# The scale of w_in from sums of squares on TensorE instead of maxima on VectorE, in a fused attention and feed-forward kernel

## The chip, the cores and the metric

The kernel runs on one core of one Trainium2 chip. The metric is device time in microseconds (us) of one execution; three executions of the kernel before are given. A core has five engines that run side by side, each through its own list of instructions in a fixed order: TensorE (PE in the profile, with its weight loads as PEld), VectorE (DVE), ScalarE (ACT), GpSimd (POOL) and SyncE (SP, which here only issues DMAs).

## The reference

Attention with a multiplicative forget gate, then a feed-forward layer, 8 batches, 8 heads, 576 positions, head width 64:

```python
scores = q @ k.T / sqrt(64)
cum = cumsum(log(clip(f, 1e-4, 1)))
attn = softmax(where(causal, -1e9, scores + cum[i] - cum[j]))
x = (attn @ v), heads side by side      # 4608 tokens x 512
h = x @ w_in                            # 512 x 1024
s = h * softmax(h)
ln = (s - mean(s)) / sqrt(var(s) + 1e-6) * g_ln
out = ln @ w_out                        # 1024 x 512
```

`w_in` and `w_out` come in 64-bit floats, everything else in 32-bit ones. So a weight is read as two 32-bit words that have to be joined into one 32-bit float.

## The kernel before, in words

**Work.** Attention is done by pairs of heads: 4 pairs per batch, 32 pairs. A pair has five tiles of query rows (i = 0 to 4, the later the longer). Per tile: score products on TensorE (`score_products`, L873, with the decay added by L869 or L871), the row maximum on VectorE (L894), the exponential with its row sum on ScalarE (L899), the reciprocal (L905, L906), the scaled probabilities (L910 or L919, recorded at the helper's line L555 for VectorE and GpSimd and L553 for ScalarE), their transposition (TensorE, L946, for the first batch, by DMA later), and the product with the values (L968 or L973), whose result goes to `x16`. After it, 36 layers of 128 tokens: product with `w_in` into `hps` (L1013), softmax and normalisation (L1022 to L1054), transposition, product with `w_out` (L1079), output. From the second batch on, and in the layers throughout, a 32-bit number is carried as two 16-bit floats, high part and rest, so a product is three passes. In the first batch the attention's products are made in 32 bits.

**The scale.** So that the 16-bit parts don't lose range, each operand is multiplied by a power of two. `scale_w_in` (L673 to L680) finds that of `w_in`: for each of the four chunks (128 x 1024 weights, 1 MB) VectorE takes the largest absolute value of the raw high words as soon as the chunk has landed (L677), then the maximum of the four (L688); TensorE turns that column into a row (L693), VectorE makes the power of two out of it (L699 to L709), TensorE spreads it to all partitions (L718), VectorE finishes it (L723, L724).

**The joining.** `weights` (L620 to L655) joins the words of chunk c: ScalarE moves the high word into place (L634), then, for chunks 0 and 1, ScalarE writes the top bits of the low word into a PSUM buffer (L648) and VectorE joins them in two halves (L654); for chunks 2 and 3 GpSimd makes the top bits (L637) and VectorE joins in one piece (L639). The joined chunk lies in a buffer of the layers (`ets`, `zts`) until it is split into `wi_h` (L665, one of three engines) and `wi_l` (L670, VectorE), which need the scale.

**The order.** Nothing is ordered on the chip. The program lists 3766 operations with their dependencies (`plan.op`); ORDER, written out by hand as numbers, says in which order each engine gets them, and ON says which of the operations that could run on several engines goes to which. An engine never passes a waiting instruction. `Plan.schedule` follows ORDER with a table of costs only to choose PSUM buffers and to find where TensorE would idle in the first 60 us: there L1204 issues products of the identity matrix that nobody reads (fillers below). TensorE uses its array either as a whole, or split by rows (scores) or columns (values, and nearly all layer products).

The operations of the start on TensorE, in order: fillers; scores of pair 0, tiles 0 to 2; fillers; the scale's transposition (L693); scores of pair 1, tiles 0 and 1; transposes of pair 0; L718; scores of pair 1, tile 2 (its products are the 64x320 ones at L873); values of pair 0; and so on to the first layer product (L1013).

The lines that matter:

```python
sw = scales["wi"][:, 1, 0:1]
copied(WI_H[c], {ACT: 1050, DVE: 690, POOL: 1130}, due, wi_h[:, c, :], w, [wk, ("scale", "wi", 0)], [("wi", c)], scale=sw)
```

Of the kernel before, what the change touches and what calls it, by code (L numbers as in the profile page):

```python
# [8 lines left out]
F32 = mybir.dt.float32  # L9
F32R = mybir.dt.float32r  # L10
I32 = mybir.dt.int32
# [4 lines left out]
ALU = mybir.AluOpType  # L16
# [68 lines left out]
class Plan:  # L85
# [140 lines left out]
    def spare(self, a, e):  # L226
# [40 lines left out]
    },  # L267
    DVE: {
# [6 lines left out]
    },  # L275
    POOL: {
        26, 67, 276, 280, 284, 613, 614, 698, 1506, 1524, 1648, 1995, 2190, 2483, 2785, 2882, 2883, 2971, 3043, 3096, 3113, 3114, 3252, 3317, 3400,
        3541, 3621, 3650, 3651, 3690,
# [156 lines left out]
def tile_kernel(ctx: ExitStack, tc: tile.TileContext, qk, v, f, w_in, w_out, g_ln, out):  # L435
# [701 lines left out]

    for p in range(NPAIR):
        load(p, -97.0 + p)
    scale_w_in(WI_SCALE)  # L1140
    load_v(0, HALF[0][0] + VDUE[0])
    for n in range(2):
        squares(0, n, 0, HALF[0][0] + VDUE[1])
# [105 lines left out]
```

## Time and profile before

| | us |
|---|---|
| median of three runs | 632.39 (631.79 to 634.35) |
| the profiled execution's own time | 630.9 |
| its span, first to last instruction | 629.1 |
| TensorE busy | 611.7 (97%) |
| VectorE busy | 570.8 (91%) |
| ScalarE busy | 516.9 (82%) |
| GpSimd busy | 347.7 (55%) |

All times in the rows are us from the start of the span unless marked ns. What lies between the span and the execution's time is 1.8 us. A matmul's record covers its whole way through the array, so records of one engine overlap: a run of equal matmuls takes the distance of their starts, not the sum of their durations. A 32-bit product shows as two records, each with a weight load of its own on PEld.

### The profile page before, as it was taken

To read this page: it belongs to the slowest core of one execution; us is meant where nothing else is said; L and a number is where in the kernel's file an instruction comes from. 1 tells how busy PE (TensorE), PEld (TensorE's weight loads), DVE (VectorE), ACT (ScalarE), POOL (GpSimd) and SP (SyncE) were. 2 spreads that over 40 slices of the span, in tenths; PEclk is the share of its full clock that TensorE was granted. 3 is DMA by queue.
4 is the path that set the end of the run, shared out by engine and by line. 5 is a ranking of instruction groups with operands and counts; after the bars stand their busy time and mean duration, and the time that the engine had idled before them with its cause. 6 is when DMAs were issued, how large, how long until landed. Compare 5 with 4: busy or idle time off the path is not lost.

```text
span 629.1 us, 20473 instructions
## 1 busy us (share of the span) xinstructions
PE 611.7 (97%) x7843; PEld 361.9 (58%) x7843; DVE 570.8 (91%) x1776; ACT 516.9 (82%) x1282; POOL 347.7 (55%) x547
## 2 busy tenths in 40 slices
PE   5899999999999999999999999999999999999997
PEld 4556665565555556555556555556655655655555
DVE  6999999999999999999999999999999999897442
ACT  6999999989989999899988889898898786764122
POOL 5565751585768646666566745664455644444230
PEclk9999999999999999999999999999999999999999
DMA  8767128979989999999999999999978687787541
GB/s 331 271 219 270 39 95 243 155 152 213 210 162 207 188 206 163 214 149 244 187 201 173 254 165 241 200 157 202 170 134 162 124 138 138 120 143 134 112 118 51
DMA packets 262722, 110.99 MB, mean 176 GB/s; under 512 B 248288, under 2 KB 248736, under 8 KB 261600
## 3 DMA queue, kind: packets, MB, share of 16 engines
q1 hardware_dynamic: 262624, 109.69, 83.9%
q8 instruction: 61, 1.00, 0.6%
q14 instruction: 37, 0.30, 0.2%
HBM read 38.27 MB, written 9.66 MB: 76 GB/s over the span
## 4 chain that ended last, share of the span: by engine, by line
PE 58%; DVE 0%; ACT 0%; issue 0%
PE ps L1079 21%; PE hps L1013 20%; PE ps L973 7%; PE ps L873 6%; PE ps L871 2%; PE ps L1093 0%; PE ps L1096 0%; PE ps L1094 0%; PE ps L693 0%; PE ps L1065 0%; PE ps L718 0%; DVE wo_p L927 0%; ACT y L1104 0%; DVE p L894 0%; DVE nm L894 0%
## 5 line engine op out<-in xcount | busy, mean ns | idle before, releaser
L1079 PE MATMUL ps<-wo_f,zz 128*64 128x512 f16 (+1 forms) x1617 | 194.0, 380 | 0.0
L899 ACT ACTIVATE p<-p,nm 128x448 f32<-128x448 f32 (+4 forms) x208 | 133.2, 642 | 15.7 <-DVE nm L894 13.4
L1079 PEld LDWEIGHTS <-zz 128*64 128x64 f16 (+1 forms) x1617 | 91.1, 109 | 84.0 <-issue 6.5
L1013 PE MATMUL hps<-wi_h,x_h 128*64 128x512 f16 (+1 forms) x562 | 111.5, 383 | 1.0 <-DVE e L1028 1.0
L1013 PE MATMUL hps<-wi_l,x_h 128*64 128x512 f16 (+1 forms) x562 | 110.3, 379 | 0.0
L1013 PE MATMUL hps<-wi_h,x_l 128*64 128x512 f16 (+1 forms) x562 | 110.3, 379 | 0.0
L873 PE MATMUL ps<-qk 64*128 64x288 f16 (+9 forms) x1056 | 101.4, 303 | 2.8 <-DMA qk<-in_qk_dram 1.8
L894 DVE CUSTOM_DVE_ANT_0 p<-ps,mask 128x320 f32<-128x320 f32 (+4 forms) x208 | 99.9, 497 | 3.6 <-PE ps L871 1.1
L1013 PEld LDWEIGHTS <-x_h 128*64 128x64 f16 (+1 forms) x1124 | 60.0, 109 | 58.1 <-issue 14.7
L1049 POOL TENSOR_TENSOR z<-e,z 128x512 f16<-128x512 f32 x55 | 66.7, 1222 | 34.2 <-ACT z L553 33.4
L927 DVE SCALAR_TENSOR_TENSOR wo_p<-p,ri,wo_p 128x448 f16<-128x448 f32 (+1 forms) x112 | 84.6, 773 | 0.7 <-ACT wo_p L553 0.3
L973 PEld LDWEIGHTS <-v 128*64 128x64 f16 x2520 | 73.1, 110 | 10.5 <-issue 2.8
L973 PE MATMUL ps<-t_p,v 128*64 128x128 f16 (+1 forms) x2520 | 76.5, 218 | 0.0
L905 POOL TENSOR_SCALAR sm<-sm 128x2 f32<-128x2 f32 (+1 forms) x93 | 29.2, 314 | 80.6 <-ACT p L899 54.9
L1024 ACT ACTIVATE e<-hps,st,unscale 128x1024 f32<-128x1024 f32 x32 | 38.5, 1203 | 27.6 <-DVE st L1023 27.4
L555 POOL TENSOR_SCALAR wo_p<-p,ri 128x576 f16<-128x576 f32 (+1 forms) x43 | 37.4, 871 | 30.4 <-DVE ri L906 21.9
L1022 DVE TENSOR_REDUCE st<-hps 128x1 f32<-128x1024 f32 x36 | 43.8, 1218 | 8.8 <-PE hps L1013 8.2
L871 PE MATMUL ps<-crow,pick 64*128 64x448 bf16 (+1 forms) x360 | 51.4, 276 | 0.0
L873 PEld LDWEIGHTS <-qk 64*128 64x128 f16 x864 | 32.4, 94 | 31.9 <-issue 20.4
L1013 PEld LDWEIGHTS <-x_l 128*64 128x64 f16 (+1 forms) x562 | 32.7, 110 | 29.5
L1036 ACT ACTIVATE junk<-e,st 128x1024 bf16<-128x1024 f32 x36 | 41.3, 1146 | 9.7 <-DVE e L1028 9.5
L1028 DVE SCALAR_TENSOR_TENSOR e<-hps,e 128x1024 f32<-128x1024 f32 x36 | 43.6, 1212 | 4.1 <-ACT e L1024 4.0
(213 smaller groups left out, 1184.5 us busy)
## 6 DMA issues: line engine op xcount, KB each, us to landing
raws<-in_qk_dram SPq DMA_DIRECT2D x24, 576.0 KB, 5.6
vraw<-in_v_dram SPq DMA_DIRECT2D x8, 1280.0 KB, 7.2
out_dram<-y SPq DMA_DIRECT2D x35, 256.0 KB, 3.1
qk<-in_qk_dram SPq DMA_DIRECT2D x8, 576.0 KB, 6.5
wo_raw<-in_w_in_dram SPq DMA_DIRECT2D x4, 1024.0 KB, 8.6
vraw<-in_w_out_dram SPq DMA_DIRECT2D x2, 1024.0 KB, 5.8
t_raw<-in_w_out_dram SPq DMA_DIRECT2D x2, 1024.0 KB, 5.5
t_p<-p16s SPq DMA_TRANSPOSE x84, 3.6
```

What stands on the lines that cost most here:

```text
L871: nc.tensor.matmul(dst, pick[row(h), a2, a1:a1 + 1].broadcast_to([D, P]), crow[row(h), a2, cols], start=False, stop=True)
L873: nc.tensor.matmul(dst, x[row(h), 0, q0:q0 + P], y[row(h), 1, cols], start=(n == 0), stop=False)
L894: op(DVE, R_NS[i] if n == 0 else 442, at[i][h] + STEPS[0], lambda i=i, h=h, n=n, a=a, e=e, x=x, m0=m0: nc.vector.tensor_tensor_reduce(home ...
L899: op(ACT, E_NS[i] + (0 if banked(p, i) or i == 4 else 28), at[i][h] + STEPS[1], lambda i=i, h=h, x=x: nc.scalar.activation(home(i, h), hom ...
L927: op(DVE, L_NS[j], at[j][g] + STEPS[4], lambda j=j, g=g, nq=nq, h16=h16, l16=l16, r1=r1: nc.vector.scalar_tensor_tensor(l16(), home(j, g, ...
L973: nc.tensor.matmul(o[row(h), a:a + n], v16[m][:, x, 2 * j + h], t[:, y, i + j if h else i - j], start=(j == 0 and c == 0), stop=(j == i an ...
L1013: nc.tensor.matmul(hps[k, sl], x[:, k], w[:, c, sl], start=start, stop=stop)
L1022: op(DVE, 1215, at, lambda: nc.vector.tensor_reduce(s[:, 0:1], hps, axis=AX.X, op=ALU.max, negate=True), [("h",)], [("st", n % 2)])
L1028: nc.vector.scalar_tensor_tensor(et, hps, 1.0 / DFF, et, ALU.mult, ALU.mult, accum_out=s[:, 3:4])
L1036: op(ACT, 1140, at, lambda: nc.scalar.activation(junk[:, :DFF], et, AF.Square, bias=s[:, 3:4], scale=-float(DFF), accum_out=s[:, 5:6]), [e ...
L1049: op(POOL, 1085, at, lambda e, a=a: engine(e).tensor_tensor(z16[:, a, 1], e2[:, a], z16[:, a, 0], ALU.subtract), [ek, zk_], [(*zk_, "l", a ...
L1079: nc.tensor.matmul(y[t], zz[:, a, x, j][:, t], wo(w, k), start=(k == 0 and n == 0), stop=(k == NFC - 1 and n == 2))
```

## The change

Four things are edited, and the order is written anew.

- L677, the maximum over a raw chunk on VectorE, is gone (four instructions of 128 x 1024 elements).
- When a chunk is joined, TensorE multiplies each of its eight 128 x 128 blocks, transposed, with itself, in 32 bits, and adds all 32 products of the four chunks in one PSUM buffer. That buffer is held from the first of them until it is read. VectorE takes the maximum of each of its rows (in place of L688's maximum of four columns). Its largest elements are sums of squares of columns, so the power of two is found by the square-root form that the other scales use already.
- The splitting into `wi_h` and `wi_l` is a function of its own, `split_w_in`. All of the joining and the scale stand ahead of the attention in the list of operations; so the scale now depends on all four joined chunks, where it depended on the raw words.
- The chain from the turned column to the power of two has one instruction less on VectorE (four after the maximum, where there were five).
- ON and ORDER are new throughout, for all 3766 operations (four fell away, four came).

```diff
+        key = ("s", "o", "gram")
+
+        def products():
+            for k in range(DFF // P):
+                x = w[:, k * P:(k + 1) * P]
+                nc.tensor.matmul(ps[plan.place[key]][:, :P], x, x, start=(c == 0 and k == 0), stop=(c == NCC - 1 and k == DFF // P - 1))
+        op(PE, 1750, due, products, [wk], [key], take=None if c else key)
+
+    def split_w_in(c, due):
+        w, wk = w_buffer(c)
...
-            op(DVE, 1220, due[0] + c, lambda c=c: nc.vector.tensor_reduce(
-                tops["wi"][:, 0, c:c + 1], buf(f"wo_{c}", "raw", 4, DM, dtype=I32).bitcast(F32).rearrange("p c (n t) -> p c n t", t=2)[:, :, :, 1],
-                axis=AX.XY, op=ALU.max, apply_absolute_value=True), [("raww", c)], [("top", "wi", c)])
+
+    def scaled_w_in(due):
         scale("wi", "wi", 0, 1, NCC, due[1])
...
+        if x == "wi":
+            op(DVE, 210, due, lambda: nc.vector.tensor_reduce(t[:, 0, NFC:], ps[plan.place["s", "o", "gram"]][:, :P], axis=AX.X, op=ALU.max), [("s", "o", "gram")], tk)
+        else:
+            op(DVE, 160, due, lambda: nc.vector.tensor_reduce(t[:, :, NFC:], t[:, :, :n], axis=AX.X, op=ALU.max),
...
-            if x == "wi":
-                nc.vector.tensor_scalar(f, f, 2.0 ** -112, None, ALU.mult)
-                nc.vector.tensor_scalar(bits, bits, 3, None, ALU.logical_shift_left)
-                nc.vector.tensor_scalar(f, f, 2.0 ** -40, None, ALU.max)
-                nc.vector.tensor_scalar(bits, bits, 0x7F800000, None, ALU.bitwise_and)
...
+            nc.vector.tensor_scalar(f, f, 2.0 ** (-80 if x == "wi" else -120), 2.0, ALU.max, ALU.mult)
+            nc.vector.tensor_scalar(bits, bits, 1, 0x7F800000, ALU.logical_shift_right, ALU.bitwise_and)
+            nc.vector.tensor_scalar(f, f, 2.0 ** 63 / (1.0 if x == "wi" else SMALL), None, ALU.mult)
...
     scale_w_in(WI_SCALE)
+    for n in range(NCC):
+        prepare_w_in(n, W_IN[0] + W_IN[1] * n)
+    scaled_w_in(WI_SCALE)
...
-        prepare_w_in(n, W_IN[0] + W_IN[1] * n)
+        split_w_in(n, W_IN[0] + W_IN[1] * n)
```

What the new numbers in ORDER and ON say, read against the new list of operations:

- TensorE: scores of pair 0, tiles 0 to 2; the products of chunks 0, 1, 2, 3, one behind the other; transposes of pair 0, tile 2; L693; transposes of tile 0; scores of pair 1, tiles 0 and 1; L718; transposes of tile 1; scores of pair 1, tile 2; then as before, with neighbours exchanged. Over the whole kernel there are 220 changes between uses of the array (whole, by rows, by columns) where there were 210, and 384 places where the next operation is of another line, where there were 362.
- VectorE: the first joins come right behind the sums of the decay, ahead of the maxima of pair 0; chunk 0 is joined before the second half of chunk 1, chunk 3 before the reciprocals of pair 0. It gets three casts of the decay (L597) and several copies of turned probabilities (L949) from ScalarE at the start.
- GpSimd: the identity matrix first; the mask (L469, L471), first before, stands behind the first parts of the decay; the top bits of chunks 2 and 3 (L637) follow it. It gets the clearing of `z` (L573) from VectorE, and gives that of `crow` (L482) to it.
- SyncE: the loads of the four chunks, the first pairs and the values as before; the small load of `g_ln` moves ahead of two loads of pairs; the second store of the decay is issued ahead of the first one's reload.
- Of the operations with a choice of engine, over the whole kernel, 98 come to VectorE and 101 leave it; 86 come to ScalarE and 96 leave it; 131 come to GpSimd and 118 leave it.
- At the end of the list on TensorE the last layer's first transposition (L1065) stands behind 12 operations of products (L1079) after the last L1013 run, where it stood behind 14, and one more of them stands between its two halves.

## Rows read from the trace of the kernel before

**Rows 1.** The page: span, busy time, share and instructions of each engine.
```profile
span 629.1 us, 20473 instructions
...
PE 611.7 (97%) x7843; PEld 361.9 (58%) x7843; DVE 570.8 (91%) x1776; ACT 516.9 (82%) x1282; POOL 347.7 (55%) x547
```

**Rows 2.** Busy time by stretches: us, then each engine's, granted clock, DMA share.
```profile
11.20:25.00 13.80, 11.47 (x122) 8.32 (x122) 13.40 (x43) 12.19 (x29) 9.58 (x13) 1.00 0.90 361
25.00:60.00 35.00, 32.99 (x325) 21.57 (x325) 32.35 (x116) 32.46 (x94) 19.77 (x27) 1.00 0.71 243
60.00:120.00 60.00, 58.09 (x603) 35.74 (x600) 57.97 (x198) 55.54 (x140) 27.10 (x50) 1.00 0.46 126
...
200.00:500.00 300.00, 299.79 (x4217) 174.76 (x4215) 290.70 (x926) 271.56 (x683) 179.85 (x278) 1.00 1.00 186
```

**Rows 3.** TensorE in order of time, the start: start, us, line, shapes, [idle before].
```profile
5.03 4.44 PE L1204 MATMUL ps<-ident 128*128 128x256 bf16 x25 [5.03 <-POOL ident masks.py:199]
11.23 0.44 PE L873 MATMUL ps<-qk 64*128 64x64 f32 x4 [1.75 <-DMA qk<-in_qk_dram]
...
13.31 3.56 PE L1204 MATMUL ps<-ident 128*128 128x256 bf16 x31
18.61 0.27 PE L693 MATMUL ps<-ident,top_wi 128*1 128x128 f32 x1 [1.74 <-DVE top_wi L688]
18.82 0.44 PE L873 MATMUL ps<-qk 64*128 64x64 f32 x4
...
19.83 0.22 PE L946 MATMUL ps<-ident,p 64*128 64x64 f32 x1
20.33 0.38 PE L718 MATMUL ps<-scale_wi,ones 1*128 1x2 f32 x2 [0.29 <-DVE scale_wi L709]
...
23.03 0.81 PE L873 MATMUL ps<-qk 64*128 64x320 f32 x4
...
34.46 0.41 PE L1013 MATMUL hps<-wi_h,x_h 128*64 128x512 f16 x2
```

**Rows 4.** Fillers (L1204) alone from 20 to 60 us: TensorE, its loads, granted clock.
```profile
20.00:60.00 40.00, 2.71 (x14) 1.20 (x14) 1.00 0.71 247
```

**Rows 5.** One line's instructions, L677 and L634: durations min/median/max in ns, first and last start.
```profile
L677 DVE TENSOR_REDUCE top_wi<-wo_raw x4: 1212/1218/1219, 7.2 to 17.2; 128x1 f32<-128x1024 f32 x4
...
L634 ACT ACTIVATE z<-wo_raw x2: 1100/1110/1119, 9.8 to 17.7; 128x1024 f32<-128x1024 f32 x2
...
L634 ACTq EVENT_SEMAPHORE  x2: 17/28/38, 13.7 to 16.2; - x2
```

**Rows 6.** 32-bit transposes by the whole array (L1065): last eight, and their weight loads.
```profile
618.03 1.09 PE L1065 MATMUL ps<-ident,z 128*128 128x128 f32 x8
...
L1065 PEld LDWEIGHTS ps<-ident,z x32: 138/140/143, 72.5 to 618.7; 128*128 128x128 f32 x32
```

**Rows 7.** VectorE in order of time around the finished scale.
```profile
21.01 0.13 DVE L724 TENSOR_SCALAR scale_wi<-ps 128x1 f32<-128x1 f32 x1
21.08 1.20 DVE L639 SCALAR_TENSOR_TENSOR z<-z,wo_raw 128x1024 int32<-128x1024 int32 x1
22.21 0.67 DVE L654 SCALAR_TENSOR_TENSOR z<-z,ps 128x512 int32<-128x512 int32 x1
```

**Rows 8.** GpSimd in order of time, the start.
```profile
0.79 0.69 POOL L469 MEMSET mask<- 128x704 bf16 x1 [0.29 <-POOLq L1236]
...
10.01 1.25 POOL L605 COPY t_cc<-t_cc 128x192 bf16<-128x192 bf16 x3 [4.25 <-DVE t_cc L598]
11.95 0.68 POOL L598 TENSOR_TENSOR t_cc<-e,t_cc 128x256 bf16<-128x256 f32 x1 [0.69 <-DVE t_cc L555]
```

**Rows 9.** The chain that ended last: two equal runs of L1013, start and us.
```profile
391.14 1.42 PE hps L1013 x12
...
401.39 1.29 PE hps L1013 x12
```

**Rows 10.** The end in order of time, TensorE and VectorE.
```profile
608.87 9.23 PE L1079 MATMUL ps<-wo_f,zz 128*64 128x512 f16 x84
...
615.68 1.00 DVE L1054 TENSOR_SCALAR z<-e,st 128x512 f32<-128x512 f32 x2 [0.61 <-POOL st L1040]
```

More of the change, by code (lines that the diff above doesn't have):

```diff
@@ L263 @@
     ACT: {
[3 rows of a table removed]
[4 rows of a table added]
     },
     DVE: {
[6 rows of a table removed]
[6 rows of a table added]
     },
     POOL: {
-        26, 67, 276, 280, 284, 613, 614, 698, 1506, 1524, 1648, 1995, 2190, 2483, 2785, 2882, 2883, 2971, 3043, 3096, 3113, 3114, 3252, 3317, 3400,
-        3541, 3621, 3650, 3651, 3690,
[3 rows of a table added]
     },
@@ L687, in scale @@
         tk, sk = [("topmost", y, j) for j in range(a, e)], [("scale", x, j) for j in range(a, e)]
-        op(DVE, 160, due, lambda: nc.vector.tensor_reduce(t[:, :, NFC:], t[:, :, :n], axis=AX.X, op=ALU.max),
-           [("top", y, c, j) if y in (0, 1) else ("top", y, c) for c in range(n) for j in range(a, e)], tk)
+        if x == "wi":
+            op(DVE, 210, due, lambda: nc.vector.tensor_reduce(t[:, 0, NFC:], ps[plan.place["s", "o", "gram"]][:, :P], axis=AX.X, op=ALU.max), [("s", "o", "gram")], tk)
+        else:
+            op(DVE, 160, due, lambda: nc.vector.tensor_reduce(t[:, :, NFC:], t[:, :, :n], axis=AX.X, op=ALU.max),
+               [("top", y, c, j) if y in (0, 1) else ("top", y, c) for c in range(n) for j in range(a, e)], tk)
         def turn():
@@ L699, in exponents @@
             nc.vector.tensor_reduce(f, ps_t(key)[:1, :m, :], axis=AX.X, op=ALU.max)
-            if x == "wi":
-                nc.vector.tensor_scalar(f, f, 2.0 ** -112, None, ALU.mult)
-                nc.vector.tensor_scalar(bits, bits, 3, None, ALU.logical_shift_left)
-                nc.vector.tensor_scalar(f, f, 2.0 ** -40, None, ALU.max)
-                nc.vector.tensor_scalar(bits, bits, 0x7F800000, None, ALU.bitwise_and)
-            else:
-                nc.vector.tensor_scalar(f, f, 2.0 ** -120, 2.0, ALU.max, ALU.mult)
-                nc.vector.tensor_scalar(bits, bits, 1, 0x7F800000, ALU.logical_shift_right, ALU.bitwise_and)
-                nc.vector.tensor_scalar(f, f, 2.0 ** 63 / SMALL, None, ALU.mult)
+            nc.vector.tensor_scalar(f, f, 2.0 ** (-80 if x == "wi" else -120), 2.0, ALU.max, ALU.mult)
+            nc.vector.tensor_scalar(bits, bits, 1, 0x7F800000, ALU.logical_shift_right, ALU.bitwise_and)
+            nc.vector.tensor_scalar(f, f, 2.0 ** 63 / (1.0 if x == "wi" else SMALL), None, ALU.mult)
             nc.vector.tensor_scalar(inv, bits, 0x7F800000, None, ALU.bitwise_xor)
```

320 rows, old and new, of tables (ON, ORDER) are left out of this document.

## The prediction, made before the change was timed

> **What bounds the kernel now.** The page first: TensorE is busy for 611.7 of 629.1 us, VectorE for 91% [rows 1]. The stretches next [rows 2]: from 200 to 500 us TensorE lacks 0.2 us of 300, so there only its own work counts, and a lighter VectorE brings nothing. What can be won lies ahead of that: 2.3 us idle of 13.8 between 11.2 and 25, 2.0 of 35 up to 60, 1.9 of 60 up to 120, with VectorE busy for 97, 92 and 97%. Third, TensorE in order of time [rows 3]: nothing useful before the first pair's load lands at 11.23; then, from 13.31 to 18.61, a hole of 5.3 us, 3.56 of fillers and 1.74 of waiting for the maxima of w_in. From 20 to 60 us there are 14 more fillers [rows 4]. At the pace of 0.115 us that the 31 in rows 3 show (3.56 / 31), they hold 1.6 us. So the change adds work to the engine that bounds the whole, and takes work from the one that bounds the start: what counts is whether the added work fits into the hole.
>
> **The change part by part.** *Removed:* four maxima of 1.22 us on VectorE, 4.9 us between 7.2 and 18.4 [rows 5]. Nothing on TensorE.
>
> *Added on TensorE:* 32 products in 32 bits of 128 x 128 by 128 columns. As each shows as two records with a load of its own, that is 64 records. No such product by the whole array is in the trace; the nearest are the 32-bit transposes of the same size [rows 6]: eight in 1.09 us, less 0.27 for a lone one's passage (L693 in rows 3), over seven steps: 0.117 us each. A chunk costs 16 x 0.117 = 1.9 us, all four 7.5 us. The lower end is the fillers' pace of 0.115 (256 columns of 16 bits, as long a stream as two passes of 128), 7.4; the upper end is loads that wait for the array, below. I take 7.5, the row of the same size and type. The granted clock of all stretches is 1.00, the 2.4 GHz level [rows 2]; that the first 25 fillers take 0.178 us each and the next 31 only 0.115 [rows 3] says that the array began at its lower level of 1.2 GHz. It did not fall back over the idle 1.75 and 1.74 us. Now the identity comes first on GpSimd, so fillers start earlier; at the lower level the products would take up to twice 7.5, nearly the price of loads in series, below.
>
> The rows of the loads say how such products overlap: each load lasts 0.140 us, longer than the pace, on the same rows of the array [rows 6], so a load runs beside the stream before it. Against that stands the Trainium skill, "TensorE: Matmul & The Clock Gate", the list "What overlaps and what doesn't" under "The mechanism": loads overlap running matmuls only where their row groups differ. By that rule load and stream would follow one another here; it is a rival below. The trace disagrees for transposes, and no run here shows a 32-bit product by the whole array yet.
>
> *Where it lies.* Products wait for joins, and TensorE passes nothing: behind them stand the transposes of pair 0, the scale's own steps and the scores of pair 1. The last chunk sets the end: ScalarE's waits for chunks 2 and 3 end at 13.7 and 16.2 [rows 5], which I take for their landing. Then L634 1.1, the join 1.2 [rows 5, 7], the products 1.9: done at 20.4. Behind it TensorE still owes what it did before 23.03 [rows 3]: L693 and the scores of pair 1, 18.61 to 19.83, 1.2 us; ten transposes at 0.117, 1.2; L718, 0.3: again 23.1, and the value product of pair 0 that used to come earlier, 0.3. So at 23 us TensorE stands **0.3 us later** than before: the hole takes 5.3 us of the products and the waits and fillers behind it the rest. The scale itself comes later: maximum 0.3, then 2.35 us from L693 to the end of L724 (18.61 to 21.14 [rows 3, 7], less one instruction of 0.18 by its neighbour's pitch): about 23.0 instead of 21.1. Behind its steps on VectorE wait two copies of turned probabilities and the maxima of pair 1; who needs the scale is the splitting of w_in, first used at 34.46 [rows 3], so 2 us are covered by 13. Were that cover gone, they would cost 2.
>
> *Moved on GpSimd:* the mask now follows three pieces of the decay. VectorE ends the last but one about 0.3 us earlier than before (1.2 us of L677 gone ahead of it, three casts of 0.3 come). Then 1.25 + 0.68 + 0.69 + 0.55 (L605, L598, mask) from about 9.7: ready at 12.9 [rows 8], where the first maximum began at 12.58. VectorE fills that time with joins. Cost 0 to 0.3, taken as 0. *On SyncE* the four loads keep their places; 4 KB of g_ln ahead of two pairs' loads, whose scores come after 25, cost nothing. The store of the decay that moves ahead of a reload frees that reload's other half earlier; crow is not read before 33, so nothing either way.
>
> *VectorE lighter:* what it saves can show only as TensorE's waits after 23 us: 2.0 and 1.9 us idle [rows 2], and 11 of the 14 fillers [rows 4], 1.2: 5.1 in all. Part of them wait for ScalarE or a chain of small steps that nothing shortens, and VectorE gets casts and copies in return. Between nothing and 5.1 I take half, **2.6 less**.
>
> *The new order:* ten more changes of the array's use. A run of L1013 entered from another use takes 1.42, the same entered from the same 1.29 [rows 9]: 0.13 each, **1.3 more** (0, if they fall into waits). *Engine choices:* as many operations come to VectorE as leave it (98, 101); beyond 120 us TensorE covers this. *The end:* the first half of the last transposition's input is ready at about 616.2, half of L1054, and TensorE comes to it at 618.03 [rows 10]. Two operations of six products fewer ahead of it (12 of 84 in 9.1 us: 1.3) leave 0.5 us. Cost 0.
>
> **The sum**: 0.3 - 2.6 + 1.3 = -1.0 on an execution of 630.9 (span 629.1 and 1.8 around it): 629.9. That execution stands 1.5 under the median of 632.39; against the median, 631.4.
>
> **The rivals.** *Start bound by VectorE:* 97% busy in all of the start speaks for it, and that the two waits on the scale, at 18.61 and 20.33, name VectorE as what ended them [rows 3]. Then all 5.1 us come back and the switches fall into waits: 0.3 - 5.1 = -4.8, 627.6. Against it: 92% from 25 to 60, and that products now hold TensorE instead.
>
> *Joins as late as before:* GpSimd, ScalarE and VectorE each bring the last chunk through a queue of attention work. Before, the last join ended at 22.88 [rows 7]. If it does again, the last product ends at 24.8 instead of 20.4 and everything behind is 4.4 later: 632.4 - 1.0 + 4.4 = 635.8, **slower**. It decides from 4.2 us, a last product after 24.6. Against it: the maxima between those joins are gone, and the joins stand ahead of more in all three lists.
>
> *Loads in series:* 64 x (0.117 + 0.140) = 16.4 us instead of 7.5. As the products of the first chunks can't start before about 12, 8.9 us would come on top: 640.3. Rows 6 speak against it.
>
> *The joins and the scale off the path, nothing won:* 0.3 + 1.3 gives 634.0; it lies within the forecast's "same".
>
> **How the numbers follow.** A measurement of this kernel can tell about 0.5% from no change, 3.2 us: faster is under 629.2, slower over 635.6. The forecast, with half, none or most of the waits returned, has 0.68, its own range 629.2 to 634.5; the start bound by VectorE 0.20; late joins 0.08; loads in series 0.04. From 627.0, a little under the second case, to 636.0, a little over the third, leaves out about 1 in 10, and 1 in 10 more for orders that I misread.
>
> **What would show it.** After the change: 64 records of the new products with a pace near 0.117, the last ending near 20.4; the scores of pair 1, tile 2, near 23; the scale done near 23, the first L1013 at 34 or before; from 25 to 120 about 2.6 us less of waits and fillers; the stretch from 200 to 500 as full as now. It is wrong if the last product ends after 24, if the products are paced at 0.2 or more, if L1013 waits for a split of w_in, or if TensorE idles by over 1 us beyond 120, where I cover the new order with nothing.

## The result and the profile after

The change is slower: 637.79 us (median of 6 runs, 635.22 to 639.26) against 633.34 (6 runs) for the kernel before beside it, a ratio of 1.007 [1.0048, 1.0092]. The forecast was 631.4, with a range to 636.0. The profiled execution has a span of 634.5 us against 629.1.

The page of the kernel after, as in [rows 1]:

```profile
PE 620.2 (98%) x7893; PEld 370.6 (58%) x7893; DVE 568.7 (90%) x1768; ACT 508.9 (80%) x1272; POOL 354.0 (56%) x560
```

Its stretches (us, then the engines' busy time, granted clock, DMA share), as in [rows 2]:

```profile
11.20:25.00 13.80, 12.50 (x128) 11.14 (x130) 8.86 (x36) 9.67 (x24) 5.85 (x11) 1.00 0.92 365
25.00:60.00 35.00, 32.90 (x327) 20.50 (x325) 33.56 (x111) 32.21 (x91) 20.23 (x30) 1.00 0.60 211
60.00:120.00 60.00, 58.46 (x607) 36.45 (x608) 55.72 (x200) 55.01 (x142) 28.74 (x55) 1.00 0.51 140
200.00:500.00 300.00, 297.57 (x4162) 173.76 (x4158) 291.76 (x927) 264.07 (x673) 187.14 (x272) 1.00 0.99 186
```

VectorE is lighter by 4.5 us from 11.2 to 25. But TensorE, idle for 0.2 us of the 300 from 200 to 500 before, now lacks 2.4 there: that is where the forecast saw nothing to lose.

The start of the kernel after, TensorE in order of time, as in [rows 3] (line numbers are shifted: L671 the new products, L707 was L693, L726 was L718, L881 was L873, L1021 was L1013):

```profile
13.51 2.05 PE L671 MATMUL ps<-e 128*128 128x128 f32 x16
15.40 1.95 PE L671 MATMUL ps<-z 128*128 128x128 f32 x16
17.19 1.95 PE L671 MATMUL ps<-e 128*128 128x128 f32 x16
20.21 2.05 PE L671 MATMUL ps<-z 128*128 128x128 f32 x16 [1.07 <-DVE z L641]
...
22.64 0.27 PE L707 MATMUL ps<-ident,top_wi 128*1 128x128 f32 x1
...
24.80 0.81 PE L881 MATMUL ps<-qk 64*128 64x320 f32 x4
...
36.73 0.41 PE L1021 MATMUL hps<-wi_h,x_h 128*64 128x512 f16 x2
```

The scores of pair 1, tile 2, begin at 24.80 instead of 23.03. Behind them stands a chain that begins with the last chunk, which ScalarE and GpSimd both wait for (same view, the two engines; then VectorE at the end of the scale):

```profile
17.70 1.14 ACT L636 ACTIVATE z<-wo_raw 128x1024 f32<-128x1024 f32 x1 [1.34 <-DMA wo_raw<-in_w_in_dram]
...
17.75 1.15 POOL L639 TENSOR_SCALAR wo_raw<-wo_raw 128x1024 int32<-128x1024 uint8 x1 [2.64 <-DMA wo_raw<-in_w_in_dram]
...
24.53 0.14 DVE L732 TENSOR_SCALAR scale_wi<-ps 128x1 f32<-128x1 f32 x1
```

The chain explains when the products end, at 22.2. It isn't the whole cause of 24.80: in edit_undone (below), which has no products, the same scores begin at 24.93, behind transposes that wait 1.27 us for GpSimd's `p` until 22.03. The chunk is as late there, so these two runs don't tell the chunk from the new order of the start.

For the rest I use a **delay**, worked out from the starts of all matmuls: how much later TensorE has done the useful work (columns streamed, without fillers and the new products) that the profiled kernel before had done at a given time. Some matmul records are missing from each trace, so it is good to about half a us. The kernel after is 2.1 us late at 25, 1.0 at 120, 1.9 at 200, 2.6 at 300, 4.5 at 400 and 5.0 at 600. So the start loses about 2 and gains half of it back by 120, and then 4 more are lost, in small pieces. Their places are in TensorE's waits beyond 120 us (line, what it waited for: us, times, longest), first the one row that before has, then the longest five of the kernel after:

```profile
PE hps L1013 <- DVE e L1028: 0.8, 1, 0.8
```

```profile
PE hps L1021 <- DVE e L1036: 1.1, 3, 0.5
PE ps L881 <- DVE nm L902: 0.7, 2, 0.4
PE ps L881 <- DVE x_l L997: 0.5, 1, 0.5
PE ps L726 <- DVE scale L724: 0.5, 1, 0.5
PE ps L881 <- DVE scale L732: 0.4, 1, 0.4
```

All five wait for VectorE, the first three for an instruction that frees a PSUM buffer. One of those in order of time, VectorE, then TensorE:

```profile
223.22 2.07 DVE L935 SCALAR_TENSOR_TENSOR wo_p<-p,ri,wo_p 128x576 f16<-128x576 f32 x2
225.22 0.81 DVE L997 SCALAR_TENSOR_TENSOR x_l<-ps,x_h 128x256 f16<-128x256 f32 x2
...
226.08 0.26 PE L881 MATMUL ps<-qk 64*128 64x64 f16 x6 [0.51 <-DVE x_l L997]
```

Two long low halves stand ahead of the two short instructions that free the buffer; one of the two takes 1.34 us, of which more below. Counting every matmul run between 120 and 600 us that starts over 0.4 us late, there are 10 of them, 5.6 us, against 1 of 1.2 before. The waits that the trace names sum to less, since a late start also holds the passage through the array.

### The profile page after: what moved, and what is told of

The parts are those of the page before. It is cut to its first block, busy times and chain, and to the rows that moved or that the text cites. A ratio compares the mean times of both kernels' runs of the same rounds, so it can differ in the third digit from the quotient of the medians.

```text
span 634.5 us, 20550 instructions
## 1 busy us (share of the span) xinstructions
PE 620.2 (98%) x7893; PEld 370.6 (58%) x7893; DVE 568.7 (90%) x1768; ACT 508.9 (80%) x1272; POOL 354.0 (56%) x560
## 4 chain that ended last, share of the span: by engine, by line
PE 68%; DVE 18%; issue 5%; ACT 4%; DMA 3%; POOL 1%; SPq 1%; DVEq 0%; POOLq 0%; ACTq 0%
PE hps L1021 22%; PE ps L1087 22%; PE ps L881 9%; PE ps L981 8%; DVE p L902 3%; PE ps L879 2%; DVE wo_p L935 2%; DMA wo_raw<-in_w_in_dram 2%; DVE qk L836 2%; DVE st L1030 2%; DVE p16s L935 2%; DVE e L1036 1%; DMA vraw<-in_w_out_dram 1%; PE ps L954 1%; DVE ps L902 1%
## 5 line engine op out<-in xcount | busy, mean ns | idle before, releaser
L1087 PE MATMUL ps<-wo_f,zz 128*64 128x512 f16 (+1 forms) x1608 | 196.2, 380 | 0.3 <-DVE nm L902 0.2
L1087 PEld LDWEIGHTS <-zz 128*64 128x64 f16 (+1 forms) x1608 | 91.3, 109 | 85.3 <-issue 8.9
L1021 PE MATMUL hps<-wi_h,x_h 128*64 128x512 f16 (+1 forms) x558 | 111.6, 383 | 1.3 <-DVE e L1036 1.3
L1021 PE MATMUL hps<-wi_l,x_h 128*64 128x512 f16 (+1 forms) x558 | 110.6, 379 | 0.0
L1021 PE MATMUL hps<-wi_h,x_l 128*64 128x512 f16 (+1 forms) x558 | 110.5, 379 | 0.0
L881 PE MATMUL ps<-qk 64*128 64x288 f16 (+9 forms) x1056 | 100.1, 303 | 2.3 <-DVE nm L902 0.7
L1021 PEld LDWEIGHTS <-x_h 128*64 128x64 f16 (+1 forms) x1116 | 60.9, 109 | 59.2 <-issue 14.6
L1057 POOL TENSOR_TENSOR z<-e,z 128x512 f16<-128x512 f32 x58 | 71.7, 1246 | 36.1 <-ACT z L555 21.7
L935 DVE SCALAR_TENSOR_TENSOR wo_p<-p,ri,wo_p 128x576 f16<-128x576 f32 (+1 forms) x112 | 85.3, 779 | 1.3 <-POOL wo_p L557 1.1
L981 PEld LDWEIGHTS <-v 128*64 128x64 f16 x2520 | 72.5, 110 | 10.1 <-issue 3.5
L981 PE MATMUL ps<-t_p,v 128*64 128x128 f16 (+1 forms) x2520 | 75.8, 218 | 0.1
L557 POOL TENSOR_SCALAR wo_p<-p,ri 128x576 f16<-128x576 f32 (+1 forms) x61 | 51.3, 844 | 29.6 <-DVE ri L914 19.3
L913 POOL TENSOR_SCALAR sm<-sm 128x2 f32<-128x2 f32 (+1 forms) x87 | 24.1, 277 | 77.1 <-ACT p L907 51.9
L1032 ACT ACTIVATE e<-hps,st,unscale 128x1024 f32<-128x1024 f32 x32 | 38.5, 1203 | 26.6 <-DVE st L1031 24.7
L881 PEld LDWEIGHTS <-qk 64*128 64x128 f16 x864 | 32.3, 94 | 33.6 <-issue 22.5
L1021 PEld LDWEIGHTS <-x_l 128*64 128x64 f16 (+1 forms) x558 | 32.9, 110 | 29.3
L907 ACT ACTIVATE ps<-ps,nm 128x64 f32<-128x64 f32 (+1 forms) x112 | 37.3, 333 | 14.5 <-DVE nm L902 13.5
L1036 DVE SCALAR_TENSOR_TENSOR e<-hps,e 128x1024 f32<-128x1024 f32 x36 | 43.8, 1217 | 4.1 <-ACT e L1032 4.0
```

The costliest lines, as they stand in the source:

```text
L557: engine(e).tensor_scalar(now(out_), now(in_), scale, by, ALU.mult, ALU.mult)
L881: nc.tensor.matmul(dst, x[row(h), 0, q0:q0 + P], y[row(h), 1, cols], start=(n == 0), stop=False)
L907: op(ACT, E_NS[i] + (0 if banked(p, i) or i == 4 else 28), at[i][h] + STEPS[1], lambda i=i, h=h, x=x: nc.scalar.activation(home(i, h), hom ...
L935: op(DVE, L_NS[j], at[j][g] + STEPS[4], lambda j=j, g=g, nq=nq, h16=h16, l16=l16, r1=r1: nc.vector.scalar_tensor_tensor(l16(), home(j, g, ...
L981: nc.tensor.matmul(o[row(h), a:a + n], v16[m][:, x, 2 * j + h], t[:, y, i + j if h else i - j], start=(j == 0 and c == 0), stop=(j == i an ...
L1021: nc.tensor.matmul(hps[k, sl], x[:, k], w[:, c, sl], start=start, stop=stop)
```

## The experiments

Two theories at first, in the letters of the expectations. **A:** two separate losses, one in the start (the late last chunk), one by the late starts that the new order and choices make beyond it. **B:** one loss in the start, which shifts everything behind it against the transfers. The runs were made in groups, each with runs of the kernel before beside it (medians 632.38 to 633.35 us), so across groups the ratios compare better than the times. ORDER and ON are long lists; in the diffs below they are written as expressions of the list before (`old`) and after (`new`), in the same names of operations. `START` is the first 900 operations of the old order (to about 115 us).

### Which half of the change

**new_start_old_rest**: the edit and the new start, the old rest.

```diff
-ORDER, ON = new
+ORDER = [n for n in new if n in START] + [n for n in old if n not in START]
+ON = {n: (new if n in START else old)[n]}
```

> The changed kernel with its own order and engine choices for the first quarter of the operations (about 115 us) and those of the kernel before for the rest. Theory A (two separate losses: about 1 to 2 us in the start, about 4 us by ten late starts on TensorE beyond 120 us that the new order makes): 1.0 to 2.0 us over the kernel before, and no wait over 0.4 us beyond 200. Theory B (one loss in the start, which shifts everything behind it against the transfers): as slow as the change, 4 to 5 us over the kernel before.

**old_start_new_rest**: the same with old and new exchanged; no edit.

> The kernel before, with the maxima on VectorE, its own order for the first quarter of the operations and the new order and engine choices for the rest. Theory A: 3 to 4 us over the kernel before, with the same late starts beyond 170 us as the change. Theory B: no difference.

**edit_undone**: the new order and choices throughout, with the four maxima on VectorE in place of the products.

> The new order and engine choices throughout, but the scale from the maxima on VectorE again (four maxima put in as the chunks land, no products on TensorE). Theory A: the start is level with the kernel before or 1 us earlier, the rest loses its 3 to 4: 2 to 4 us over the kernel before, 1 to 3 under the change. Theory B: level with the kernel before.

| run | us | ratio |
|---|---|---|
| new_start_old_rest | 632.84 | 0.9994 [0.9979, 1.0009] |
| old_start_new_rest | 638.28 | 1.0076 [1.0055, 1.0097] |
| edit_undone | 638.57 | 1.0088 [1.0059, 1.0116] |

B falls, and the second loss of A is there twice over: with the rest alone exchanged, the change gets 637.79 - 632.84 = 4.95 us shorter, and the kernel before 638.28 - 633.33 = 4.95 longer (633.33 is the median of before beside these runs). The first loss of A doesn't show in the times: the edit with its start is level with before, where A expected 1 to 2 us over it, and taking the edit out (edit_undone) makes the change no faster, where A expected 1 to 3 us. What is exchanged is the lists of all engines, and with them the choice of PSUM buffers; VectorE's list was not exchanged by itself. TensorE's waits beyond 120 us of new_start_old_rest:

```profile
PE hps L1019 <- DVE e L1034: 0.8, 1, 0.8
PE ps L879 <- issue: 0.5, 1, 0.5
```

The row that before has too, and one more; old_start_new_rest has most of the change's list back, at the same instructions some 2 us later.

### Order or choices

**rest_new_choices**: new start, then the old order with the new engines. **rest_new_order**: new start, then the new order with the old engines.

```diff
-ON = {n: (new if n in START else old)[n]}
+ON = new
```

> New start as in the run before it; behind it the old order with the new choices of engines. If the loss of 5 us behind the start lies in the choices: 637 to 638. If it lies in the order in which VectorE and TensorE take their work: 633 to 634, few starts late by over 0.4 us beyond 120.

> New start; behind it the new order with the old choices of engines. If the loss lies in the choices: 633 to 634. If it lies in the order: 637 to 639, with the same late starts as the change. If in both together, in the fit of one to the other: both of these runs slower than the change's 638.

653.26 us, ratio 1.0336 [1.0309, 1.0362], and 663.83, 1.0497 [1.0472, 1.0521]. Both mixtures are far worse than either kernel, as the last of the expectations had it: order and choices fit each other, and the 5 us can't be split between them.

### The start

**fewer_fillers** (of the change) and **start_fewer_fillers** (of new_start_old_rest):

```diff
-FILLED = ((0.0, 13.5, 0.85),
+FILLED = ((0.0, 13.5, 0.45),
```

> The change with about half of the fillers ahead of 13.5 us, so that TensorE's next 16 KB of code are loaded later than 15.0 us, when the last chunk has landed. If that load held the chunk up (16.4 to 17.7 us) and the chunk set the end of the products: landing near 16.4, products done near 20.8 instead of 22.1, and 1 us less in all. If the products or the joins set it by themselves: the products done near 22, no difference. If the array drops to its lower level without the fillers: products twice as long, slower by several us.

> New start, old rest, and half of the fillers ahead of 13.5 us. If the code load at 15 us holds up the last chunk and this the whole start: 1 to 2 us under the new start with the old rest (632.8), so 631 to 632, and faster than the kernel before by 1.5 to 2 us. If the start is bound otherwise: 632.8.

**start_one_block** (of new_start_old_rest):

```diff
-            for k in range(DFF // P):
-                x = w[:, k * P:(k + 1) * P]
+            x = w[:, :P]
```

> New start, old rest, with one of the eight blocks of each chunk multiplied (the other seven are left out of the sums, so the scale differs). The products then take 0.9 us instead of 7.5. If their work is what the start pays: about 1.7 us less behind the last chunk, 631. If the wait for the last chunk's join and the chain of small steps behind the products set it: less than 1 us, 632 to 633. If the products cost all of their 6.6 us on the path: 626.

With fewer fillers the change takes 635.92 us (1.0037 [1.002, 1.0053]; the intervals just overlap), new_start_old_rest 632.15 (0.9998 [0.9979, 1.0016]), no difference that can be told from its 632.84. In fewer_fillers the last packets of the last chunk came 1.4 us earlier, but the delay at 23 us was 2.0, no smaller; in both runs the granted clock was 0.79 from 12 to 20 us. That the clock took what the earlier chunk gave is my reading; no run has the early chunk with a full clock. That fewer_fillers is still 1.9 us under the change, with a start as late, stays without a cause; the change's own runs spread over more than that. With one block of eight, 635.15 us (1.0042 [1.0026, 1.0059]), slower than with all eight. Its stretches from 12 to 30 us, and two runs of TensorE:

```profile
12.00:20.00 8.00, 3.03 (x37) 2.04 (x33) 5.67 (x18) 5.63 (x16) 3.99 (x7) 0.82 1.01 405
20.00:30.00 10.00, 9.42 (x57) 6.41 (x59) 5.05 (x30) 6.52 (x19) 1.96 (x3) 0.50 0.67 244
```

```profile
19.95 0.80 PE L668 MATMUL ps<-z 128*128 128x128 f32 x2 [3.09 <-DVE z L639]
...
26.31 1.44 PE L878 MATMUL ps<-qk 64*128 64x320 f32 x4
```

The granted clock falls at 17.1 us, behind a wait of 1.88 us for a join and early in the next one, of 3.09, and is 0.50 from 20 to 30 us, the 1.2 GHz level; the run that takes 0.81 us in the kernel after takes 1.44. So the products' 7.5 us cost this start no more than leaving the hole empty would. The hole is empty here because fillers are laid out by the table of costs, in which an operation of products keeps its full price. Against a hole full of fillers only edit_undone compares, and it is level with the change.

### What in the rest

Three theories now. **C: place.** Single instructions stand too late in VectorE's list. **D: load.** VectorE has no slack, and in the new rest it is busy for longer ahead of the same work of TensorE. **E:** the late starts are an effect, and TensorE's own work the cause. For D speaks a second curve of the same kind: by the time that TensorE has done what before had done at 120 us, VectorE has been busy 5.1 us less in the change than in before, but at 360 us only 0.2 less; in new_start_old_rest the lead stays between 4.6 and 5.1.

**change_again**: the change once more, as a neighbour.

> The change itself, once more, as the neighbour of nine_moves on the same chip. Both theories: about 1.007 of the kernel before, 637.8 us, and the same ten late starts of TensorE by over 0.4 us between 120 and 600 us, 5.6 us in all.

**nine_moves**: VectorE's list alone, nine instructions moved; for the place shown above (p16l is a low half of L935, x_l an L997, by pair and tile):

```diff
-p16l 11/4, p16l 11/4, x_l 10/1, x_l 11/0
+p16l 11/4, x_l 10/1, x_l 11/0, p16l 11/4
```

> The change with nine of VectorE's instructions moved, and nothing else: the lists of the other engines are the change's. In seven places beyond 170 us the instruction that TensorE was seen to wait for stands one or two places earlier, ahead of a long one (the low halves of L935, the maximum L1030, the split of v L846) that nobody waits for so soon, wherever its own inputs were there by then; one small step of the gate's chain (L1040) moves behind two row maxima. Those waits of the change are 0.33 (178.6), 0.51 (226.1), 0.24 (231.8), 0.35 (247.3), about 0.2 of 0.65 (311.0), 0.47 (358.5) and 0.30 us (531.3): 2.4 us. If the loss lies in where VectorE's order puts these instructions, the waits go and the time falls by some 2 us, to about 635.5, ratio about 1.0035. If VectorE is short of time as a whole in the new order, so that what is moved ahead makes something else late, waits of the same size come back at other places and the time stays at 637.8 within 0.5. If the late starts are an effect and not the cause (the loss sits in TensorE's own work), they go and the time stays.

**vector_lighter** (of the change):

```diff
+            few = 64 if j == 4 and 9 <= p < 17 else w
...
-nc.vector.scalar_tensor_tensor(l16(), home(j, g, nq), r1, h16(), ALU.mult, ALU.subtract)
+nc.vector.scalar_tensor_tensor(l16()[:, :few], home(j, g, nq)[:, :few], r1, h16()[:, :few], ALU.mult, ALU.subtract)
```

> The change with 16 of VectorE's long instructions cut short: the low halves of the widest turned probabilities (L935, 128 x 576, 0.81 us each) of the pairs 9 to 16, which fall between 190 and 310 us, are written for 64 of their 576 columns alone, some 0.15 us. The rest of those columns keeps what an earlier pair left there. That takes about 16 x 0.66 = 10.6 us of work from VectorE and nothing from any other engine. If the new order's loss between 160 and 360 us is that VectorE, busy for 98 of 100 us there, has to do more ahead of the same work of TensorE, the late starts from 226 to 358 us go and the time falls by 2 to 3.5 us, to 634 to 636, ratio 1.001 to 1.004; later late starts (437 to 441, 531) stay. If single misplaced instructions or TensorE's own work are the cause, it stays at 637.5 (ratio 1.007) within 0.7.

**vector_heavier** (of new_start_old_rest):

```diff
+for _ in range(2 if j == 4 and 9 <= p < 17 else 1):
     nc.vector.scalar_tensor_tensor(l16(), home(j, g, nq), r1, h16(), ALU.mult, ALU.subtract)
```

> The other way round: the new start with the old rest (632.8 us, level with before), in which the same 16 instructions are each issued twice in a row: 16 x 0.81 = 13.0 us more work for VectorE, with the same result, and nothing more for any other engine. VectorE was 4.7 us ahead of the kernel before at 200 us, and idle for 2.0 us of 100 from there to 300 and 3.8 to 400. If VectorE is a second bound there, hidden under TensorE by a few us, the time grows by what is not covered: 13.0 less 4 to 9 us of slack, 4 to 9 us, to 637 to 642, by late starts of TensorE that wait for VectorE, as in the change. If a heavier VectorE is covered by TensorE from 200 to 500 us, as the prediction had it, the time stays at 632.8 within 0.7.

**vector_lighter_all** (of the change) and **old_rest_lighter** (of new_start_old_rest):

```diff
-            few = 64 if j == 4 and 9 <= p < 17 else w
+            few = 64 if j == 4 and p >= 6 else w
```

> The change with 52 of VectorE's instructions cut short instead of 16: the low halves of the widest turned probabilities (L935, 128 x 576) of all pairs from 6 on are written for 64 of 576 columns alone, from about 138 us to the end: 52 x 0.66 = 34 us of VectorE's work less, of some 453 between 120 and 600 us; the rest of the columns keeps what earlier pairs left. If VectorE's load is the cause of the loss all over the rest, the late starts shrink in all stretches and the time comes to within 1 us of old_rest_lighter, 632 to 634. If single waits of the new order are late whatever the load, those at 177, 357, 438 and 531 us stay, and the time stays at 635.5 to 637.5.

> The new start with the old order and choices for the rest (632.8 us), with the same 52 instructions cut short. It has only three late starts beyond 110 us, 1.5 us in all. If TensorE covers VectorE in the old rest, the time is the same, 632 to 633; if VectorE's load costs something there as well, it falls, by at most those 1.5 us, to 631.3.

**nine_moves_lighter**: the edits of nine_moves and of vector_lighter_all together. **more_moves**: at full load, eight of the nine moves and five more.

> The change with the nine moves of nine_moves and the 52 short instructions of vector_lighter_all (most of the columns of these low halves keep what earlier pairs left). If the loss is misplaced instructions on a VectorE that has no slack, the two together do what neither did alone: the waits of 178 to 358 and 531 us go and no others come, the late starts fall from 6 to about 3 us, those of 116 and 437 to 441 us being left, and the time falls to about 634.5 (ratio 1.003). If neither load nor place on VectorE is the cause, it stays at 637 to 638.5.

> The change at full load with the moves of nine_moves but one (531 us is left as it was) and five more on VectorE: the spread of the scale (L731, L732) ahead of two low halves of 1.9 us, a row maximum ahead of the maximum L1030, and two splits of raw q and k near 428 us ahead of a low half and a row maximum, so that the buffer of the next load comes free some 1.1 us earlier. The other engines' lists are the change's. If the loss is a matter of single places that can be mended one after the other, the waits of nine_moves at 245 and 247 us (1.9 us) go, those of 437 to 440 us (1.6 us) shrink by about 1, and the time falls to 634.5 to 635.5. If a VectorE without slack makes something else late for each wait that is mended, it stays at 637 to 638.5.

The growth of the delay from 120 to 520 us and the late starts over 0.4 us between 120 and 600, both of the profiled execution:

| run | us | ratio | delay grows by | late starts, us |
|---|---|---|---|---|
| the change | 637.79 | 1.007 [1.0048, 1.0092] | 3.5 | 10, 5.6 |
| change_again | 637.45 | 1.0067 [1.0045, 1.0089] | 5.5 | 11, 8.0 |
| nine_moves | 638.78 | 1.0071 [1.0045, 1.0097] | 3.4 | 7, 6.1 |
| vector_lighter | 636.9 | 1.0049 [1.003, 1.0068] | 4.7 | 11, 7.1 |
| vector_lighter_all | 637.33 | 1.0058 [1.0033, 1.0083] | 4.0 | 9, 6.2 |
| nine_moves_lighter | 635.93 | 1.0051 [1.0027, 1.0075] | 1.3 | 6, 4.0 |
| more_moves | 637.63 | 1.0076 [1.0052, 1.01] | 4.3 | 9, 6.9 |
| new_start_old_rest | 632.84 | 0.9994 [0.9979, 1.0009] | 0.9 | 2, 1.8 |
| old_rest_lighter | 633.89 | 1.0013 [1.0001, 1.0025] | 1.9 | not counted |
| vector_heavier | 649.46 | 1.025 [1.0229, 1.0271] | 16.9 | not counted |

By the times, none of the runs with the new rest can be told from the change (ratios from 1.0049 to 1.0076, with intervals that overlap), nor old_rest_lighter from new_start_old_rest. What is said of them below rests on one profile each.

**vector_heavier** is the plainest: 13.0 us more for VectorE made the kernel 649.46 - 632.84 = 16.6 us longer, more than was put in and well over the 4 to 9 that I expected. The stretch from 200 to 300 us, of new_start_old_rest and of it:

```profile
200.00:300.00 100.00, 99.80 (x1442) 58.66 (x1439) 98.00 (x311) 93.26 (x242) 62.50 (x96) 1.00 0.98 194
200.00:300.00 100.00, 90.79 (x1316) 54.56 (x1314) 98.76 (x294) 83.07 (x217) 57.78 (x85) 1.00 0.89 169
```

TensorE's first waits beyond 120 us:

```profile
PE ps L879 <- DVE p16s L935: 3.4, 3, 1.7
PE ps L879 <- DVE nm L900: 3.1, 3, 1.7
PE ps L879 <- DVE x_l L998: 2.2, 2, 1.3
```

TensorE falls to 90.8 of 100 us, with VectorE as full as ever. So in the old rest, too, VectorE is a second bound: none of what was added at these places was covered.

**The other way it is not so simple.** In old_rest_lighter nothing is won (633.89 against 632.84). In the change, VectorE lighter by 10.6 us between 190 and 310 takes the growth of the delay out of 200 to 280 us (0.0 there, 1.0 in the change and in change_again), and the later stretches keep theirs; lighter by some 34 us all over, some waits stay as they were. vector_lighter_all, the stretch from 300 to 400 us:

```profile
300.00:400.00 100.00, 98.41 (x1315) 56.74 (x1313) 93.23 (x304) 89.77 (x220) 62.26 (x92) 1.00 0.95 193
```

Its first waits of TensorE beyond 120 us:

```profile
PE hps L1022 <- DVE e L1037: 1.4, 3, 0.7
PE ps L707 <- DVE top L702: 1.0, 1, 1.0
PE ps L1088 <- DMA zz<-z: 0.8, 1, 0.8
```

VectorE is busy for 93 of 100 us now, and TensorE still waits for L1037: that instruction stands behind other long ones, whatever the load of the rest. So less load alone does not mend it.

**Nor do other places alone.** nine_moves loses the three waits on L1036 that it was made against; the first waits of its trace, where L979 and L1085 are the lines L981 and L1087 of the change:

```profile
PE ps L979 <- DVE nm L900: 1.1, 2, 0.9
PE ps L879 <- DVE scale L730: 1.1, 1, 1.1
PE ps L1085 <- DMA zz<-z: 0.8, 1, 0.8
PE ps L705 <- DVE top L700: 0.8, 1, 0.8
```

Others have come in their place, at 245, 247, 437 and 533 us, and the time is the same. more_moves loses the rows of L730 and L705, and gets 3.2 us of waits on L900 instead.

**Both together** leave 1.3 us of growth to 520 us, against 0.9 in the old rest. That looks like C and D combined, but it isn't shown. Up to 430 us the delay grows by about 2.4 us with the moves alone and by 2.0 with both; most of the rest of the difference is one wait at 437 us, of which the next paragraph tells and which two profiles of the change itself differ by. From 520 to 600 us both grow by over 1 us more. And of the late starts that nine_moves brought, those at 245, 247 and 533 us are there with both, the first half as long: the moved places don't hold on a lighter VectorE either. The ratio, 1.0051, went only half of the way to the expected 1.003. Against E speaks only that the delay moves with VectorE's work at all, as in vector_heavier.

Part of what is left is no engine's own. In change_again, at 437 us, TensorE waits 1.5 us for the maximum of the squares of q and k, which ScalarE makes late (ScalarE in order of time):

```profile
436.37 1.16 ACT L743 ACTIVATE junk<-raws 128x1152 bf16<-128x1152 f32 x1 [3.05 <-DMA raws<-in_qk_dram]
```

The load of raw q and k is issued at about 430 us, right behind the split on VectorE that frees its buffer. In the first profile of the change the same wait was 0.51 us and cost TensorE 0.2. Such a chain (VectorE, a transfer, ScalarE, VectorE, TensorE) stands or falls with a few tenths, which may be why the change's runs spread over 635 to 641 us.

**What none of these runs changed.** In the new rest the same instructions of VectorE last longer. The stretch from 120 to 600 us, before and after:

```profile
120.00:600.00 480.00, 478.86 (x6543) 277.73 (x6541) 451.03 (x1393) 404.90 (x1003) 279.74 (x424) 1.00 0.94 175
```

```profile
120.00:600.00 480.00, 476.06 (x6492) 277.04 (x6489) 453.04 (x1392) 395.55 (x993) 291.00 (x432) 1.00 0.94 175
```

VectorE has about as many instructions as before and is busy for 2.0 us more; GpSimd is busy for 11.3 us more, ScalarE for 9.4 less. I compare each of VectorE's instructions of this stretch with the shortest of the same operation, tile and shape in any run. In before 18 of them last over 0.25 us longer than that, 10.0 us in all; in the change 32, 19.6 us. It is 18 in new_start_old_rest too, and 29 to 34 in all runs with the new order and choices there; nine_moves_lighter still has 32 of them, 19.5 us. Every one of these runs beside an instruction of GpSimd. That alone is not enough, since 72% of VectorE's instructions do and most last no longer. An example, ahead of the late start at 358.5 us, VectorE, GpSimd, then TensorE of the kernel after:

```profile
353.28 2.52 DVE L836 SCALAR_TENSOR_TENSOR qk<-raws,scale,qk 128x576 f16<-128x576 f32 x2
355.72 1.58 DVE L935 SCALAR_TENSOR_TENSOR wo_p<-p,ri,wo_p 128x448 f16<-128x448 f32 x1
357.22 1.21 DVE L1036 SCALAR_TENSOR_TENSOR e<-hps,e 128x1024 f32<-128x1024 f32 x1
...
353.52 3.29 POOL L1057 TENSOR_TENSOR z<-e,z 128x512 f16<-128x512 f32 x2
...
358.50 0.41 PE L1021 MATMUL hps<-wi_h,x_h 128*64 128x512 f16 x2 [0.47 <-DVE e L1036]
```

Of the first form the shortest take 0.78 us, of the second 0.65. The low half of 1.34 us ahead of the late start at 226.08 is another such, of 0.78 us at its shortest. So the longer busy VectorE of D comes at least in part from what GpSimd does beside it, which a count of VectorE's operations can't show. No run changes this alone, so what part of the 5 us it makes is not shown.

**Open:** how much of the 5 us is load, how much is place, and how much is VectorE's instructions lasting longer beside GpSimd. A kernel that beats the one before by more than can be told was not found; the lowest median is that of start_fewer_fillers, 632.15, level with it.

## Why the prediction was wrong

The step that failed is "*Engine choices:* as many operations come to VectorE as leave it (98, 101); beyond 120 us TensorE covers this". It was costed at nothing; order and choices beyond the start together measured 4.95 us, in both swaps. What it rested on failed first: "from 200 to 500 us TensorE lacks 0.2 us of 300, so there only its own work counts, and a lighter VectorE brings nothing". The second half is right (old_rest_lighter), but it does not follow that a VectorE with the same work in another order costs nothing: VectorE is busy for 290.7 of those 300 us [rows 2], and in vector_heavier more work for it is not covered. Two engines were the bound there, and I counted operations that came and went instead of asking what VectorE has to finish before each thing that TensorE waits for, and how long it takes for that beside the others: 14 more of its instructions last over 0.25 us longer than need be. By which of these the late starts come about stays open. I had named the sign of it ("if TensorE idles by over 1 us beyond 120, where I cover the new order with nothing") and given it no case of its own among the rivals.

The other steps:

- *The products, 0.117 us each, 7.5 in all.* Right. Sixteen records in 2.05 us, less 0.27 for one's passage, over 15 steps: 0.119. The loads last 0.19 us each here, longer than the pace, so they run beside the streams. The rival of loads in series, from the Trainium skill, "TensorE: Matmul & The Clock Gate", "What overlaps and what doesn't" under "The mechanism", is ruled out for this case: the trace now has such products by the whole array, and it disagrees with that rule.
- *Last chunk 16.2, products done 20.4, +0.3 at 23 us.* The chain was right and its first term wrong: landing at 17.7, products done at 20.21 + 1.95 = 22.2, and +1.8 (24.80 for 23.03). Why the chunk is late is under the last heading. But the path has a second holder that I left out: without any products (edit_undone) the scores come as late, at 24.93, behind GpSimd's `p`.
- *The scale at 23.0, covered by the 13 us ahead of the first L1013.* It was ready at 24.7; L1021 starts at 36.73 and waits for nothing of it.
- *VectorE lighter, -2.6.* Too much: the delay falls by 1.1 from 25 to 120 us in the change, and by 0.9 in new_start_old_rest.
- *The new order's switches, +1.3.* Not where I put them. In the traces the changes of the array's use are 150 beyond 120 us, where before has 148; between 25 and 120 they are 67 for 55, and there the delay falls all the same, by the 1.1 above. What they cost by themselves is not shown.
- *The end, 0.* Right: the delay is 5.0 at 600 us and 4.6 at the end.

By terms, in one profile: 2.1 at 25 us, less 1.1, 4.0 more from 120 to 600, less 0.4, are 4.6 of the 5.4 us by which its span is longer. The first two don't show in the median of new_start_old_rest; the last paragraph has a possible reason.

## What to carry over

Where one engine is full, look at the next one: an engine busy for 98 of 100 us under a full TensorE had no room for more work here, and a rewritten order has to be read against what it must finish before each wait, not by counts of operations. Compare how long the same instruction lasts in both kernels, since an engine can get slower without getting more to do. Change an edit and an order separately; here the edit was level, and the order that came with it cost 5 us. The late waits mended in VectorE's full list were replaced by others; look at the delay curve of the whole, not at the wait.

## What was not expected of the hardware

**A packet of the instruction queue stood ahead of the last chunk.** DMA queues of the kernel after, 14 to 18 us (queue: packets, MB, share of 16 engines; then a transfer issued behind the chunks, KB, us to landing):

```profile
q8 instruction: 1, 0.02, 1.7%
...
c_scratch<-t_cc SPq DMA_DIRECT2D x1, 108.0 KB, 12.5
```

The same of the kernel before, where no such packet falls into that stretch (its first comes between 21 and 24 us):

```profile
c_scratch<-t_cc SPq DMA_DIRECT2D x1, 108.0 KB, 11.7
```

1.7% of 16 engines over 4 us is 1.1 us on one of them: the packet, of 16 KB, runs from 15.04 to 16.11. Of the 512 packets of the four chunks all but two have ended by 15.94; the last two start at 16.10 and 16.90 and end at 16.9 and 17.2, where before has its last end at 15.7. That they wait on the same DMA engine is inferred from these times. That the packet is code of TensorE is inferred too: the first of the kind comes behind 243 matmuls and weight loads in before, 227 in the change and 212 in fewer_fillers, and so, with more fillers and products, 7 us earlier than in before. In fewer_fillers it came at 19.3, and the chunk ended at 15.8.

**The spread of the kernel before goes with the clock in its start.** Its 23 runs beside new_start_old_rest go with their mean granted clock: 630.8 us at 1.000, 631.7 to 633.0 at 0.997, 634.3 to 635.9 at 0.989 to 0.992. (The 22 runs of another group are less clean: 630.8 to 633.5 at 0.997.) The profile that I predicted from was one at 1.00. new_start_old_rest ran at 1.000 in 11 of 12, though its own profile is 1.9 us longer than that one. A TensorE that is kept busy in the start may be what evens out the two; start_one_block, which leaves its hole empty, ran at 0.989 to 0.994 and 635.15 us. The products aren't needed for it: edit_undone, with fillers in their place, ran at 1.000 in 4 of 6.
